# Converting eight instead of five float64 weight blocks during the attention

## The chip, the cores and the metric

The kernel runs on one core of a Trainium2 chip. The metric is the device time in microseconds (us) of one execution; the time of a kernel is the median of a few runs. Besides the times there is a profile of one execution: a page of views and a trace that can be queried. Engines are called as in the profile: PE is TensorE (PEld its weight loads), DVE is VectorE, ACT is ScalarE, POOL is GpSimd, and SP is SyncE, which issues most of the DMAs.

## The reference

Three stages follow one another: an attention with four sink keys and a window of 128 keys, a two-layer MLP with a PReLU, and a layer of eight experts with top-1 routing.

```
x = attention(q, k, v)              # 2 batches x 8 heads x 768 tokens x 64
x = x as (1536 tokens, 512)
h = x @ w_in                        # 512 -> 2048
g = max(h, 0) + alpha * min(h, 0)
x = g @ w_out                       # 2048 -> 512
e = argmax(x @ w_gate)              # one of 8 experts per token
out = gate * (max(x @ w1[e], 0) @ w2[e])
```

`w_in` and `w_out` come as float64; all the rest is float32.

## The kernel before

**Weights.** [...] Each of the two matrices is cut into eight blocks of 128x1024 values; the order of work is `wi0, wo0, wi1, wo1, ...`, sixteen blocks numbered 0 to 15. A block passes through three functions. `w_load` issues its DMA of 1 MB (1024 KB in the profile) on SP's queue into one of two raw buffers (two halves of `raw_all`). `w_convert` makes float32 of it: ACT takes an absolute value (L211 or L229), then DVE runs four instructions, a maximum (L216), a shift with a mask (L219), and two that merge bits of the high word (L224) and of the low word (L231). `w_convert_n(n)` converts block n and then issues the load of block n + 2, since the raw buffer is then free. `w_split` cuts the float32 block into a high and a low part, because every product is made of three float32r matmuls: ACT copies the high part (L259), and DVE or POOL subtracts (L262).

**Attention.** 48 units (2 batches x 4 pairs of heads x 6 query tiles of 128) go through a software pipeline written out by hand: pass n of a loop does the scores of unit n (L722, and all that belongs to it) together with the softmax of unit n - 1 (L737 on DVE, L741 on ACT), the transposes of unit n - 2 (L754), the product with the values of unit n - 6 (L832), the normalisation of two units that are 7 and 8 back (L843 to L850 on DVE), and two passes after that the transposes of the normalised tile (L797), which ACT and POOL (L811) then store as `x`. There are 59 passes; from pass 48 on no new unit enters, and the pipeline drains. In these last passes the first eight steps of the MLP are woven in (`next(mlp)`), four for each of its first two hidden tiles. Six units share one set of `ka` and `qa` tiles; SP loads the set of units 12 to 17 in pass 6, with two buffers for each.

**Early weights.** `early_weights` is a generator which converts blocks 0 to 4 during the attention, each in two halves, with seven stops per block. `EARLY = 32` lets it advance by one stop in each pass from n = 16 (48 - 32) on. The loads of blocks 0 and 1 are issued in passes 8 and 14. The first three blocks are also split there, the subtraction on POOL. SP's queue in the first passes further holds eight DMAs (`FILL_AT`) that write zeros to the table `xs` in device memory, 771 KB each.

**MLP.** Four blocks of tokens (512, 512, 256, 256), each with 16 hidden tiles f. Step f does 12 matmuls up (L350), 12 matmuls down for tile f - 2 (L381, in the first two blocks of tokens), and the activation: ACT L361 and L362, DVE L363, ACT L370, DVE L373. In the first block of tokens step f also converts weight block f + 3 (from f = 2 on) and splits weight block f + 2; later blocks of tokens only split. DVE works in the order of the program, in each such step: L216, L219, L363, L224, L231, L262, L373.

Of the kernel before, what the change touches and what calls it, by code (L numbers as in the profile page):

```python
# [35 lines left out]
def attention_mlp_moe_kernel(  # L36
# [19 lines left out]
    B, _, _, S = q.shape  # L56
    _, NG, _, GH, NQ, D1 = v.shape
# [130 lines left out]
    def w_load(n):  # L188

        if n >= len(worder):  # L190
            return
        nm, fg = worder[n]
        if nm == "wi":
            src = w_in_v[:, :, fg * FG * P * EW:(fg + 1) * FG * P * EW]
        else:
            src = w_out_v[:, fg * FG:(fg + 1) * FG, :]
        if wide_w:
            t = raw_all[:, n % 2 * 2 * SW:(n % 2 + 1) * 2 * SW]
        else:
            t = wres[nm, fg] = slot(f"{nm}{fg}", F32)  # L200
        nc.sync.dma_start(out=t.rearrange("p (a b) -> p a b", a=src.shape[1]), in_=src)
        wraw[nm, fg] = t

    def w_convert(nm, fg, parts=1):

        raw = wraw[nm, fg].rearrange("p (n t) -> p n t", t=2)
        lo, hi, hif = raw[:, :, 0], raw[:, :, 1], raw.bitcast(F32)[:, :, 1]
        w = wres[nm, fg] = slot(f"{nm}{fg}", F32)
        wb = w.bitcast(I32)
        cuts = [slice(o, o + SW // parts) for o in range(0, SW, SW // parts)]  # L210
        nc.scalar.activation(w[:, cuts[0]], hif[:, cuts[0]], AF.Abs)  # L211
        if parts > 1:
            yield
        for n, x in enumerate(cuts):

            nc.vector.tensor_scalar(  # L216
                out=w[:, x], in0=w[:, x], scalar1=TINY, scalar2=None, op0=ALU.max
            )
            nc.vector.tensor_scalar(  # L219
                out=wb[:, x], in0=wb[:, x], scalar1=3, scalar2=0x3FFFFFF8,  # L220
                op0=ALU.logical_shift_left, op1=ALU.bitwise_and,
            )
            yield
            nc.vector.scalar_tensor_tensor(  # L224
                out=wb[:, x], in0=hi[:, x], scalar=-0x40000000, in1=wb[:, x],
                op0=ALU.bitwise_and, op1=ALU.bitwise_or,
            )
            if n + 1 < parts:
                nc.scalar.activation(w[:, cuts[n + 1]], hif[:, cuts[n + 1]], AF.Abs)  # L229
            yield  # L230
            nc.vector.scalar_tensor_tensor(  # L231
                out=wb[:, x], in0=lo[:, x], scalar=29, in1=wb[:, x],
                op0=ALU.logical_shift_right, op1=ALU.bitwise_or,
            )
            if parts > 1:
                yield

    def w_convert_n(n, parts=1):

        if wide_w and n < len(worder):  # L240
            yield from w_convert(*worder[n], parts)
            w_load(n + 2)

    def w_split(n, parts=1):


        bl, m = divmod(n, len(worder))
        if bl >= NBLK:
            return
        nm, fg = worder[m]  # L250
        w = wres[nm, fg]
        r = 2 * (fg % 2) + (4 if nm == "wo" else 0)
        hi, lo = slot(f"r{r}"), slot(f"r{r + 1}")
        a = KD if nm == "wi" else FG
        wts[bl, nm, fg] = [t.rearrange("p (a b) -> p a b", a=a) for t in (hi, lo)]
        eng = nc.gpsimd if parts > 1 else nc.vector
        xs_ = [slice(o, o + SW // parts) for o in range(0, SW, SW // parts)]
        for x in xs_:
            nc.scalar.copy(hi[:, x], w[:, x])  # L259
            yield  # L260
        for x in xs_:
            eng.tensor_sub(lo[:, x], w[:, x], hi.bitcast(F32)[:, x])  # L262
            if parts > 1:
                yield
# [57 lines left out]
    ahead = wide_w and shared and NT // XB > 1 and PW <= 2 * P + 8  # L322
# [5 lines left out]
    def open_first():  # L328
        gp.append(mctx.enter_context(tc.tile_pool(name="gp", bufs=2, side="right")))
        slots_m = mctx.enter_context(tc.tile_pool(name="slots_m", bufs=1, side="right"))  # L330
        for n in (2, 3):
            slot_pool[f"r{n}"] = slots_m

    if ahead:
        open_first()
        for tag in ("wi2", "wo2"):
            slot_pool[tag] = slots_x

    nalpha = const.tile([P, KF], F32, name="nalpha")
# [45 lines left out]

    def convert_at(n):

        return iter(()) if ahead and n < 2 else w_convert_n(n + 3)

    def split_at(n):  # L390

        return iter(()) if ahead and n < 1 else w_split(n + 2)

    LAG = 2
    three = ((0, 0), (0, 1), (1, 0))


# [92 lines left out]
    def mlp_steps():  # L490
# [7 lines left out]
        def lower(part=None):  # L498
            pb, pf, pg = pending[0]
            ts = range(TBLK[pb][1] // P)  # L500
            if pf == 0:
                accs[pb] = [bank("t", f"acc{pb}_{t}", (P, DM)) for t in ts]
            mlp_down(pb, pf, wts[pb, "wo", pf // FG], pg, accs[pb], ts)
            pending.pop(0)
            if pf < KF - 1:
                return None
            routing = route(pb, ts, accs[pb], [])
            next(routing)
            return routing
# [4 lines left out]
        def down_to(t):  # L514

            for pb, pf, pg in pending:
                if pf not in first_down:
                    first_down.append(pf)
                    mlp_down(pb, pf, wts[pb, "wo", pf // FG], pg, accs[pb], [t])

        for bl in range(NBLK):
# [4 lines left out]
            for f in range(KF):  # L526
# [5 lines left out]
                if last and f == KF - 1:  # L532
                    down_to(0)
                elif len(pending) == LAG:
                    routing = lower() or routing
# [72 lines left out]
    with ExitStack() as actx:  # L608
# [264 lines left out]

        def early_weights():
            split = iter(())
            for n in range(5 if ahead else 0):
                for _ in w_convert_n(n, 2):
                    yield
                    next(split, None)
                for _ in split:  # L880
                    pass
                split = w_split(n, 2) if n < 3 else iter(())
            for _ in split:
                pass

        nu = len(units)
        assert NQ % 2 == 0 and NQ >= 6

        def at(xs, n):
            return xs[n] if 0 <= n < len(xs) else None  # L890
# [6 lines left out]
        for st in sts[1:QA]:  # L897
            load_qk(st)
        early = early_weights()
        nc.sync.dma_start(out=alpha_sb, in_=alpha)  # L900
        nc.sync.dma_start(out=wg_sb, in_=w_gate)
# [1 line left out]

        EARLY, MLP_AHEAD = 32, 8

        FILL_AT = (3, 5, 7, 10, 12, 15, 18, 20)

# [4 lines left out]
        for n in range(nu + 11):  # L914
            u = at(units, n)
            norm = iter(())
            if n % 2 == 0 and at(groups, (n - 8) // 2):
                norm = normalise(groups[(n - 8) // 2])
            if at(units, n - 1):
                softmax(units[n - 1], norm)  # L920
            for _ in norm:
                pass
            parts = {"T": p_transposes(units[n - 2]) if at(units, n - 2) else iter(())}
            parts["V"] = values(units[n - 6]) if at(units, n - 6) else iter(())
            for h in range(2):
                parts["QR"[h]] = scores(u, h) if u else iter(())
            for x in WEAVE:
                next(parts[x], None)
            for x in "TQRV":
                for _ in parts[x]:  # L930
                    pass
            if at(units, n - 2):
                p_evacuate(units[n - 2])
            if n % 2 == 0:
                late_transposes(at(groups, (n - 4) // 2), at(groups, (n - 10) // 2))
            elif at(groups, (n - 3) // 2):
                sink_gather(groups[(n - 3) // 2])
            if u:
                st = u.t.st
                sn = st.b * (H // 2) + st.hp  # L940
                s2 = at(sts, sn + 2)
                if u.i == 0 and sn > 0 and at(sts, sn + QA - 1):
                    load_qk(sts[sn + QA - 1])
                if u.i == 1 and st.hp % 2 == 0 and s2:
                    load_v(s2.b, s2.hp // 2)
            if n in FILL_AT:
                next(table, None)
            if ahead and n in (nu - EARLY - 8, nu - EARLY - 2):
                w_load(int(n > nu - EARLY - 8))
            if n == nu - EARLY:  # L950
                nc.vector.tensor_scalar(
                    out=nalpha, in0=alpha_sb, scalar1=-1.0, scalar2=None, op0=ALU.mult
                )
            if n >= nu - EARLY:
                next(early, None)
            if n >= nu and ahead and n_ahead < MLP_AHEAD:
                next(mlp)
                n_ahead += 1
# [433 lines left out]
```

## Time and profile before

| what | before |
|---|---|
| median of 3 runs | 612.49 us (611.35 to 613.03) |
| profiled execution | 612.21 us, its span 610.4 us |
| PE busy | 587.4 us (96%) |
| DVE busy | 396.6 us (65%) |
| ACT busy | 346.6 us (57%) |
| mean granted clock of PE | 0.997 |
| DMA | 81.76 MB, 134 GB/s on average |

The span reaches from the first to the last instruction of the profiled execution; its own time has 1.8 us more around it. PE is nearly always busy, but its matmuls are pipelined and a matmul that waits inside the pipeline also counts as busy, so idle time of PE and the distance between the starts of its matmuls are read together. The attention fills the first 122 us or so, the first block of tokens of the MLP the stretch to about 204 us.

### The profile page before, as it was taken

Reading aid. Unit: us, or ns where it says so; the run is one execution under the profiler, and the core shown is the slowest. Engines: PE = TensorE matmul, PEld = TensorE weight load, DVE = VectorE, ACT = ScalarE, POOL = GpSimd, SP = SyncE. Lnnn points to the kernel's source line nnn. Section 1 sums busy time; section 2 is a strip of 40 time slices with the busy share of each in tenths; the row PEclk is TensorE's granted clock in tenths of the full one; section 3 lists DMA queues with packets and bytes.
Section 4 is the critical chain, followed back from the end, with each engine's and each line's share of the span. In section 5 each row is a group of like instructions: output and inputs, shape, how many; then the busy total and the mean of one; then the engine's idle time right before and its main releaser. Section 6 shows DMA issues by size and latency. Waiting matters only on the chain. (4 is left out here: it accounts for less than half of the span.)

```text
span 610.4 us, 9113 instructions
## 1 busy us (share of the span) xinstructions
PE 587.4 (96%) x3230; PEld 491.7 (81%) x3230; DVE 396.6 (65%) x788; ACT 346.6 (57%) x642; POOL 100.0 (16%) x134
## 2 busy tenths in 40 slices
PE   7999999999989999999999999999999999999994
PEld 5999998888767888888899898877777777778783
DVE  5678788589999454454565786976326583985250
ACT  4677776476565354434564676854327574675330
POOL 5011423210000000003000020112220431332031
PEclk9999999999999999999999999999999999999998
DMA  7969741225559000001000011334928593993000
GB/s 220 327 206 300 226 126 70 70 69 169 176 159 389 4 0 1 2 0 53 17 1 2 18 67 35 127 99 128 335 69 307 200 356 126 310 381 141 17 21 34
DMA packets 32404, 81.76 MB, mean 134 GB/s; under 512 B 3574, under 2 KB 4134, under 8 KB 32352
## 3 DMA queue, kind: packets, MB, share of 16 engines
q1 hardware_dynamic: 28208, 69.54, 34.6%
q0 software_dynamic: 4144, 11.53, 5.2%
q8 instruction: 31, 0.51, 0.3%
q14 instruction: 21, 0.17, 0.1%
HBM read 66.65 MB, written 16.29 MB: 136 GB/s over the span
## 5 line engine op out<-in xcount | busy, mean ns | idle before, releaser
L350 PE MATMUL h<-x,r 128*128 128x512 f32 (+1 forms) x768 | 149.2, 341 | 3.2 <-DVE r L262 3.1
L350 PEld LDWEIGHTS h<-x,r 128*128 128x128 f32 x768 | 120.1, 189 | 22.3 <-DVE r L262 5.2
L381 PE MATMUL acc<-r,gh 128*128 128x512 f32 x384 | 120.5, 395 | 0.0
L381 PEld LDWEIGHTS acc<-r,gh 128*128 128x128 f32 x384 | 69.9, 188 | 14.3
L381 PE MATMUL acc<-r,gl 128*128 128x512 f32 x192 | 75.9, 395 | 0.0
L363 DVE SCALAR_TENSOR_TENSOR g<-gn,nalpha,g 128x512 f32<-128x512 f32 (+1 forms) x64 | 39.3, 615 | 47.6 <-ACT g L362 47.6
L722 PE MATMUL s<-ka,qa 128*128 128x260 f32 x192 | 60.3, 401 | 4.5 <-DMA qa<-in_q_dram 4.2
L361 ACT ACTIVATE gn<-h 128x512 f32<-128x512 f32 (+1 forms) x64 | 31.4, 490 | 53.6 <-PE h L350 53.4
L832 PEld LDWEIGHTS o<-vr,pT 128*128 128x128 f32 x352 | 55.6, 192 | 4.8
L1104 POOL DMA_INDIRECT xs<-x,slot_i x12 | 14.0, 1166 | 272.1 <-DVE run L1120 151.2
L262 DVE TENSOR_TENSOR r<-wo,r 128x1024 fp32r<-128x1024 f32 x31 | 37.9, 1224 | 27.6 <-ACT r L259 27.4
L832 PE MATMUL o<-vr,pT 128*128 128x65 f32 x352 | 53.6, 251 | 0.0
L1219 ACT ACTIVATE hh<-et 128x512 f32<-128x512 f32 x26 | 15.6, 599 | 65.3 <-PE et L1214 58.8
L741 ACT ACTIVATE p<-sx,mn 128x260 f32<-128x260 f32 (+1 forms) x96 | 42.9, 487 | 10.1 <-DVE mn L737 9.6
L259 ACT CAST r<-wo 128x1024 fp32r<-128x1024 f32 (+1 forms) x33 | 33.8, 1023 | 22.6 <-PE acc L381 21.7
L754 PE MATMUL pt<-ident,p 128*128 128x128 f32 x176 | 46.5, 279 | 0.0
L737 DVE CUSTOM_DVE_ANT_0 sx<-s,mask 128x260 f32<-128x260 f32 (+1 forms) x96 | 36.8, 399 | 14.4 <-PE s L722 8.7
L370 ACT CAST gh<-g 128x512 fp32r<-128x512 f32 (+1 forms) x64 | 33.0, 516 | 20.9 <-DVE g L363 20.7
L381 PEld LDWEIGHTS acc<-r,gl 128*128 128x128 f32 x192 | 36.1, 188 | 8.6
L262 DVE TENSOR_TENSOR r<-wi,r 128x1024 fp32r<-128x1024 f32 x30 | 36.6, 1222 | 3.6 <-ACT r L259 3.4
L373 DVE TENSOR_TENSOR gl<-g,gh 128x512 fp32r<-128x512 f32 (+1 forms) x64 | 35.3, 551 | 1.6 <-ACT gh L370 1.6
L722 PEld LDWEIGHTS s<-ka,qa 128*128 128x128 f32 x192 | 31.2, 201 | 5.6 <-issue 4.2
(200 smaller groups left out, 1104.0 us busy)
## 6 DMA issues: line engine op xcount, KB each, us to landing
raw_all<-in_w_dram SPq DMA_DIRECT2D x36, 512.0 KB, 5.9
more_raw<-in_w_dram SPq DMA_DIRECT2D x28, 512.0 KB, 6.5
raw_all<-in_w_in_dram SPq DMA_DIRECT2D x8, 1024.0 KB, 5.4
raw_all<-in_w_out_dram SPq DMA_DIRECT2D x8, 1024.0 KB, 5.7
xs<-r SPq DMA_DIRECT2D x8, 771.0 KB, 10.6
rows<-xs POOLq DMA_DIRECT2D x20, 256.0 KB, 5.7
vr<-in_v_dram SPq DMA_DIRECT2D x4, 780.0 KB, 5.5
out_dram<-fill SPq DMA_DIRECT2D x2, 1536.0 KB, 11.4
```

The source lines that it names most:

```text
L259: nc.scalar.copy(hi[:, x], w[:, x])
L262: eng.tensor_sub(lo[:, x], w[:, x], hi.bitcast(F32)[:, x])
L350: nc.tensor.matmul(ph[:, :TB], wi[wl][:, kk, f0:f0 + P], xT_at(kk, tok, TB, xl), start=(n == 0), stop=(n == 3 * KD - 1),)
L363: nc.vector.scalar_tensor_tensor(out=g, in0=gn, scalar=nalpha[:, f:f + 1], in1=g, op0=ALU.mult, op1=ALU.add)
L370: nc.scalar.copy(gh, g)
L373: nc.vector.tensor_sub(gl, g, gh.bitcast(F32))
L381: nc.tensor.matmul(acc[t], g[a][:, t * P:(t + 1) * P], wo[w][:, f % FG, :], start=(f == 0 and x == 0), stop=(f == KF - 1 and x == 2),)
L722: nc.tensor.matmul(s[:, o:o + w], st.qa[:, h, toks], st.ka[:, c:c + w], start=True, stop=True, skip_group_check=True,)
L737: nc.vector.tensor_tensor_reduce(out=x[:, :w], in0=u.s[h][:, :w], in1=m[:, :w], scale=-scale, scalar=BIG, op0=ALU.add, op1=ALU.min, accum_ ...
L741: nc.scalar.activation(t.p[:, u.ii, h, :w], x[:, :w], AF.Exp, bias=t.mn[:, c:c + 1], scale=-1.0)
L754: nc.tensor.transpose(pt[:, c * P:(c + 1) * P], t.p[:, u.ii, h, u.offs[n]:u.offs[n] + P], ident,)
L832: nc.tensor.matmul(t.o[:, 2 * u.ii + h, :], u.pT[:, w], vr[:, hv * NQ + j, :], start=(not sg and n == 0), stop=(n == len(js) - 1), skip_gr ...
```

## The change

Eight blocks instead of five are converted in the attention: `LEAD = 6` replaces the 3 in `convert_at`, and `early_weights` runs over `LEAD + 2` blocks. It starts at pass 10 instead of 16 (`EARLY = 38`) and advances by two stops in each pass from n = 48 on. The loads of blocks 0 and 1 hang on the same constant and so are issued in passes 2 and 8. Blocks 8 to 15 are left to the MLP, in its steps f = 2 to 9. Two more slots (`wi3`, `wo3`) are taken from the pool that exists during the attention.

```
-        for tag in ("wi2", "wo2"):
+        for tag in ("wi2", "wo2", "wi3", "wo3"):
             slot_pool[tag] = slots_x
...
-        return iter(()) if ahead and n < 2 else w_convert_n(n + 3)
+        return iter(()) if ahead and n < 2 else w_convert_n(n + (LEAD if ahead else 3))
...
     LAG = 2
+
+    LEAD = 6
...
-            for n in range(5 if ahead else 0):
+            for n in range(LEAD + 2 if ahead else 0):
                 for _ in w_convert_n(n, 2):
...
-        EARLY, MLP_AHEAD = 32, 8
+        EARLY, MLP_AHEAD = 38, 8
...
-            if n >= nu - EARLY:
+            for _ in range((n >= nu - EARLY) + (n >= nu)):
                 next(early, None)
```

The two loads outside the generator stand in the same loop and are not edited: `if ahead and n in (nu - EARLY - 8, nu - EARLY - 2): w_load(...)`.

## Rows read from the trace of the kernel before

**Rows 1.** The page: its head, and the rate of the DMAs in 40 slices.
```profile
span 610.4 us, 9113 instructions
...
GB/s 220 327 206 300 226 126 70 70 69 169 176 159 389 4 0 1 2 0 53 17 1 2 18 67 35 127 99 128 335 69 307 200 356 126 310 381 141 17 21 34
```
**Rows 2.** Waits of PE, whole span: us in total, times, longest us.
```profile
PE h L350 <- DVE r L262: 3.1, 4, 0.9
...
PE pk_x L797 <- DVE xn L850: 0.9, 1, 0.9
```
**Rows 3.** Timeline of PE, late steps of the first MLP block: start us, us.
```profile
179.95 0.62 PE L350 MATMUL h<-x,r 128*128 128x512 f32 x2
181.31 2.56 PE L350 MATMUL h<-x,r 128*128 128x512 f32 x10 [0.74 <-DVE r L262]
...
192.02 0.63 PE L350 MATMUL h<-x,r 128*128 128x512 f32 x2
193.56 2.60 PE L350 MATMUL h<-x,r 128*128 128x512 f32 x10 [0.91 <-DVE r L262]
...
204.43 2.91 PE L350 MATMUL h<-x,r 128*128 128x512 f32 x12
```
**Rows 4.** Timeline of DVE, the same instruction in two steps running.
```profile
158.61 0.75 DVE L363 SCALAR_TENSOR_TENSOR g<-gn,nalpha,g 128x512 f32<-128x512 f32 x1
...
164.74 0.74 DVE L363 SCALAR_TENSOR_TENSOR g<-gn,nalpha,g 128x512 f32<-128x512 f32 x1
```
**Rows 5.** Busy us in one stretch: PE, PEld, DVE, ACT, POOL, then clock, DMA.
```profile
155.00:196.00 41.00, 37.88 (x161) 29.50 (x159) 40.59 (x48) 24.79 (x34) 0.00 (x0) 1.00 0.67 233
```
**Rows 6.** Waits of DVE: two of 109.9 to 126.7 us, then one of 40 to 123.
```profile
DVE g L363 <- ACT g L362: 5.3, 2, 3.0
DVE den L843 <- PE o L832: 1.5, 1, 1.5
...
DVE wi L216 <- ACT wi L211: 2.4, 2, 1.3
```
**Rows 7.** Timeline of DVE, second half of weight block 4.
```profile
109.89 0.41 DVE L216 TENSOR_SCALAR wi<-wi 128x512 f32<-128x512 f32 x1
110.33 0.83 DVE L219 TENSOR_SCALAR wi<-wi 128x512 int32<-128x512 int32 x1
111.20 0.69 DVE L224 SCALAR_TENSOR_TENSOR wi<-raw_all,wi 128x512 int32<-128x512 int32 x1
...
112.63 0.68 DVE L231 SCALAR_TENSOR_TENSOR wi<-raw_all,wi 128x512 int32<-128x512 int32 x1
```
**Rows 8.** Timeline of POOL at the same place.
```profile
110.14 0.74 POOL L811 TENSOR_TENSOR x<-xn,x 128x256 fp32r<-128x256 f32 x1 [2.70 <-ACT xn L810]
```
**Rows 9.** Timeline of PE: first scores of units 12, 18 and 24.
```profile
27.09 0.60 PE L722 MATMUL s<-ka,qa 128*128 128x260 f32 x2
...
40.48 0.60 PE L722 MATMUL s<-ka,qa 128*128 128x260 f32 x2
...
53.89 0.60 PE L722 MATMUL s<-ka,qa 128*128 128x260 f32 x2
```
**Rows 10.** Timeline of SP, issues of DMAs in passes 6 to 8.
```profile
14.14 2.53 SPq L695 DMA_DIRECT2D qa<-in_q_dram  x2
16.72 0.61 SPq L155 DMA_DIRECT2D xs<-r  x1
17.37 0.60 SPq L201 DMA_DIRECT2D raw_all<-in_w_in_dram  x1
```
**Rows 11.** DMA issues at 14.1, 15.4, 16.8, 17.4 us: KB, us to landing.
```profile
qa<-in_q_dram SPq DMA_DIRECT2D x1, 192.0 KB, 10.4
...
qa<-in_q_dram SPq DMA_DIRECT2D x1, 192.0 KB, 9.8
...
xs<-r SPq DMA_DIRECT2D x1, 771.0 KB, 10.6
...
raw_all<-in_w_in_dram SPq DMA_DIRECT2D x1, 1024.0 KB, 12.8
```

## The prediction, made before the changed kernel ran

> **What bounds the kernel now.** I read the page first, then PE's list of waits, then the first block of the MLP and the attention one engine at a time, and last the DMA issues. The reader is to see that PE sets the end nearly everywhere, and that the conversions matter at one place. PE's list of waits has one entry that a conversion causes: four waits of the up matmuls for the low part of a split `wi` block (L262), 3.1 us in all [rows 2]. They lie in the first block of tokens, at f = 8, 10, 12 and 14. There DVE has more work per step than PE. DVE's period is 164.74 - 158.61 = 6.13 us [rows 4], and it is busy for 40.59 of 41 us [rows 5]; PE needs, without a wait, (204.43 - 193.56 + 0.48) / 2 = 5.7 us for a step [rows 3], where 0.48 us stands for the two matmuls that run ahead of the wait (12 in 2.91 us, 0.24 each). So DVE falls behind by 0.45 us a step from f = 2 on, first eats its lead, and from f = 8 on PE pays at every second step, when a new `wi` block is due. The two later payments are 181.31 - 179.95 - 0.48 = 0.88 us and 193.56 - 192.02 - 0.48 = 1.06 us [rows 3], 1.9 us together.
>
> In the attention PE is the bound and the conversions cost nothing: six units take 40.48 - 27.09 = 13.39 us almost without conversions and 53.89 - 40.48 = 13.41 us with them [rows 9]. That holds as long as DVE's instructions fit beside the softmax, as they do at one stop per pass.
>
> **The change, part by part.**
>
> *Steps f = 10 to 12 lose their conversion.* Steps f = 2 to 9 still convert, eight instead of eleven, so DVE falls behind in the same way up to f = 9. The low part that is due at f = 10 is made in step 8, behind seven conversions, before as after. What goes are the waits at f = 12 and 14: a gain of 1.9 us. The waits at f = 8 and 10 stay. More than the 3.1 us of all four waits [rows 2] is not to be had here, and whatever makes DVE arrive later at f = 2 is passed on in full to the up matmuls at f = 10, since DVE has no idle time in between.
>
> *The last passes of the attention get DVE work.* With one stop per pass from n = 10, blocks 0 to 4 end in pass 44 and three stops of block 5 in pass 47. At two per pass, the rest of block 5 falls into passes 48 and 49, block 6 into 50 to 53 and block 7 into 53 to 56. For DVE that is five half blocks and one L231. A half block costs 0.41 + 0.43 + 0.69 + 0.68 = 2.2 us by durations [rows 7], with L219 undisturbed as below, 2.1 us as the starts overlap a little; so 5 x 2.1 + 0.65 = 11.1 us come. What leaves these passes is the second half of block 4, 0.41 + 0.83 + 0.69 + 0.68 = 2.6 us [rows 7], now done six passes earlier. Net 8.5 us. DVE's room there is its waits, 5.3 + 1.5 = 6.8 us [rows 6]. Not all of it can be used: in pass 50 the two calls issue ACT's absolute value of block 6 and DVE's maximum that reads it, one behind the other, and DVE stands in line until ACT is through the copies of that pass. The longest such wait in the trace is 1.3 us [rows 6]; I take 1.0. So 8.5 - 5.8 = 2.7 us do not fit, and with half a collision with POOL more (below), DVE reaches f = 2 about 2.9 us late. Bounds: 1.2 us (halves at 2.0 us, all 6.8 us used) and 4.4 us (halves at 2.2 us, the 1.3 us wait, two more collisions of 0.4 us). Queued behind these DVE instructions are the last normalisation, for which PE already waits 0.9 us [rows 2] and will wait about 1 us longer, and the activations of tiles 0 and 1. PE's own loss there is not added: it lies inside the 2.9 us, which come due at f = 6 to 10 anyway.
>
> Both parts together: 2.9 - 1.9 = +1.0 us (-0.7 to +2.5).
>
> *The start at pass 10 instead of 16.* The pattern of early stops against the six units of a set is the same, shifted by exactly one set, so I take blocks 0 to 4, their splits and their collisions at no cost; the cover is PE's 13.4 us per set [rows 9]. Had DVE no room there, each block would cost up to its 4.2 us.
>
> *The loads of blocks 0 and 1 in passes 2 and 8.* They pass other DMAs on SP's queue. The load of pass 2 is now issued ahead of two zero fills and ahead of `ka` and `qa` of units 12 to 17. The DMAs of this queue land in the order of issue: the fill issued at 16.72 lands at 27.3, the load issued at 17.37 at 30.2 [rows 10, 11]. Thus the megabyte itself takes 2.9 us, and `qa`, landed now at 14.14 + 10.4 = 24.5 us and, its second half issued 1.2 us later, at 15.3 + 9.8 = 25.1 us, would land at 27.4 and 28.0. The scores need the first half at 27.09 [rows 9] and the second 0.66 us later. So PE loses 0.3 to 0.4 us, and nothing behind gives it back, since PE is the bound there. The other end: at the mean rate of the first slice, 220 GB/s [rows 1], the megabyte takes 4.8 us and PE loses 2.1 us. If the fills give way, nothing. I take 0.5 us, near the row of the load itself. The load of pass 8 stands where that of block 0 stood, and the later ones come between loads with more slack; nothing for these.
>
> Sum: +1.0 + 0.5 = +1.5 us. The profiled execution took 612.21 us (span 610.4 [rows 1], 1.8 around it), so 613.7; the median of the runs lies 0.28 us above that execution, so 614.0 us against the median.
>
> **A rule weighed.** L219 takes 0.83 us beside the POOL instruction of 110.14 us and 0.43 alone [rows 7, 8]: a collision costs 0.4 us of the 0.74 that POOL works. The Trainium skill, SBUF — State Buffer, section "SBUF: two separate sides", says more: the port pair of VectorE and GpSimd is an exclusive lock held for a whole instruction, and the loser blocks entirely. By the row one more collision is 0.4 us; by the rule it can be the full 0.74, which in this trace no L219 of 110 us shows, because POOL had started 0.2 us before it.
>
> **The rivals.**
>
> *Faster: DVE's gaps swallow the tail.* If DVE comes to f = 2 on time, because its waits of the last passes [rows 6] are room in full and ACT hands over without delay, and if the early load hides, the waits at f = 12 and 14 go for nothing in return: -1.9 us, 610.6; if 1.0 us is left over, 611.6. For it: 6.8 us of room stand against 8.5 us of work. Against it: the room has to lie where the work is. It decides for "faster" only when less than about 0.1 us is left over, which is why most of this case is "same". Chance 0.22 (0.14 faster, 0.08 same).
>
> *Slower by far: POOL blocks DVE in the tail.* Passes 50 to 56 hold four POOL instructions of 0.74 us like the one of [rows 8], now each beside a conversion. If each stops DVE for its whole length, the tail grows by 4 x 0.74 = 3.0 us instead of my 0.2: +4.3 us, 616.8. Against it: most conversions in the attention meet POOL without PE losing anything. Chance 0.10, slower. This is the case of the rule above.
>
> *The early load is hidden.* If the megabyte of pass 2 overlaps with the fills or a set of `qa` is not late, only +1.0 us is left: 613.5. Chance 0.15 (0.14 same).
>
> **Chances and range.** My forecast has 0.53. A measurement of this kernel can tell about 0.3%, 1.84 us, from no change: 610.65 to 614.33. The forecast lies inside, near the upper edge, with its own range 612.6 to 615.8; I put 0.31 of it on "same" and 0.22 on "slower". Together: faster 0.14, same 0.31 + 0.08 + 0.14 = 0.53, slower 0.22 + 0.10 + 0.01 = 0.33. The range 611.0 to 616.4 leaves out the better half of the first rival and most of the second, about 0.2.
>
> **What would show it right or wrong.** In the profile after: a wait of PE's scores for `qa` near 27 us of some tenths; the sets of six units after it again at 13.4 us; no DVE wait of a microsecond between 113 and 127 us except one for ACT's L211; the last L797 about 1 us later; a first PE wait for L262 already at f = 6, further ones at f = 8 and 10 of about 1 us, and none after; the up matmuls of the second token block at about 206 us instead of 204.43. I am wrong if DVE still shows free microseconds in the last passes (then faster), if the scores of unit 12 wait for 1 to 2 us or DVE instructions there stretch beside POOL (then slower).

## The result and the profile after

The changed kernel took 615.17 us (median of 8 runs, 613.97 to 617.16) against 612.13 us for the kernel before (8 runs, 611.06 to 613.03). The ratio is 1.0059, with a 95% interval of 1.0046 to 1.0071: 3.6 us slower by the ratio (the two medians alone differ by 3.0). The span of the profiled execution is 613.9 us instead of 610.4. Lines of the attention and behind it stand two further down than before (L722 is L724, L797 is L799, L811 is L813, L850 is L852).

PE's list of waits after, over the whole span (us in total, times, longest):

```profile
PE pk_x L799 <- DVE xn L852: 2.5, 1, 2.5
...
PE h L350 <- DVE r L262: 2.0, 3, 0.9
PE s L724 <- DVE xn L852: 1.0, 1, 1.0
```

Beside [rows 2], three things are to be seen. The waits for a low part fell from four to three, and from 3.1 to 2.0 us. The wait of the last transpose grew from 0.9 to 2.5 us. And a new wait stands ahead of scores. The timeline of PE shows that it is the first scores of unit 12; those of units 18 and 24 follow below it, and the last scores of unit 11 stand above:

```profile
26.52 0.60 PE L724 MATMUL s<-ka,qa 128*128 128x260 f32 x2
...
28.67 0.68 PE L724 MATMUL s<-ka,qa 128*128 128x260 f32 x2 [0.97 <-DVE xn L852]
...
42.14 0.60 PE L724 MATMUL s<-ka,qa 128*128 128x260 f32 x2
...
55.54 0.60 PE L724 MATMUL s<-ka,qa 128*128 128x260 f32 x2
```

Against [rows 9] unit 12 is 1.58 us late and unit 24 is 1.65 us late; the two sets between take 13.47 and 13.40 us, so the loss is carried through the attention as it is. Not all of it is a wait. In the trace of before, the last scores of unit 11 started here:

```profile
26.07 0.60 PE L722 MATMUL s<-ka,qa 128*128 128x260 f32 x2
```

PE was thus 0.45 us late already ahead of unit 12. It was as late at 10.19 us (9.74 before), when the early load had not been issued yet, so this part is a difference between two executions and not of the change: in the thirteen profiles of this case these scores start anywhere from 24.86 to 26.52 us. From there to unit 12 it is 28.67 - 26.52 = 2.15 us instead of 27.09 - 26.07 = 1.02, and 1.13 us is the wait.

What ended the wait is `qa`. The profile puts it down to DVE's `xn`, which ended at 28.65 us, but `xn` is a result of the attention that the scores do not read. In the profile of a later run with the same order of DMAs (spare matmuls for PE, below) the same wait carries the name of `qa`:

```profile
28.16 0.68 PE L724 MATMUL s<-ka,qa 128*128 128x260 f32 x2 [1.44 <-DMA qa<-in_q_dram]
```

These are SP's issues of DMAs after (start, time to issue), and then the KB and the time to landing of the load, of the second fill, of `ka` and of the first `qa`:

```profile
11.27 0.42 SPq L201 DMA_DIRECT2D raw_all<-in_w_in_dram  x1
11.88 1.78 SPq L155 DMA_DIRECT2D xs<-r  x2
14.19 0.93 SPq L692 DMA_DIRECT2D ka<-in_k_dram  x1
15.16 1.29 SPq L697 DMA_DIRECT2D qa<-in_q_dram  x2
```
```profile
raw_all<-in_w_in_dram SPq DMA_DIRECT2D x1, 1024.0 KB, 9.3
...
xs<-r SPq DMA_DIRECT2D x1, 771.0 KB, 13.0
...
ka<-in_k_dram SPq DMA_DIRECT2D x1, 396.0 KB, 14.0
qa<-in_q_dram SPq DMA_DIRECT2D x1, 192.0 KB, 13.4
```

The first `qa` lands at 15.16 + 13.4 = 28.56 us, just ahead of the scores, instead of 14.14 + 10.4 = 24.54 [rows 10, 11]: 4.0 us later, not 2.9.

The end of the attention and the first steps of the MLP, on PE's timeline:

```profile
125.08 0.41 PE L799 MATMUL pk_x<-ident,xn 128*128 128x128 f32 x2 [2.48 <-DVE xn L852]
125.25 4.59 PE L350 MATMUL h<-x,r 128*128 128x512 f32 x12
...
132.49 2.97 PE L350 MATMUL h<-x,r 128*128 128x512 f32 x12
...
150.17 2.60 PE L350 MATMUL h<-x,r 128*128 128x512 f32 x10 [0.38 <-DVE r L262]
...
162.43 2.58 PE L350 MATMUL h<-x,r 128*128 128x512 f32 x10 [0.76 <-DVE r L262]
...
174.68 2.62 PE L350 MATMUL h<-x,r 128*128 128x512 f32 x10 [0.90 <-DVE r L262]
...
179.94 2.97 PE L350 MATMUL h<-x,r 128*128 128x512 f32 x12
...
207.87 2.88 PE L350 MATMUL h<-x,r 128*128 128x512 f32 x12
```

The lines are the start of f = 2 behind the last transpose, f = 3, the waits at f = 6, 8 and 10, step f = 11, and the second token block. The waits stand at f = 6, 8 and 10 and nowhere after. The second token block (the last line) begins at 207.87 us instead of 204.43 [rows 3], 3.44 us late, and that distance stays to the end of the span (3.5 us). In the trace of before, the up matmuls of f = 2 and of f = 11 are these:

```profile
122.03 3.05 PE L350 MATMUL h<-x,r 128*128 128x512 f32 x12
...
174.32 2.97 PE L350 MATMUL h<-x,r 128*128 128x512 f32 x12
```

One thing was not foreseen: the twelve up matmuls of f = 2 took 4.59 us instead of 3.05. The windows of after give the reason (us of the stretch, busy us and instructions of PE, PEld, DVE, ACT, POOL, then the granted clock, and the DMAs' share and GB/s):

```profile
120.00:123.00 3.00, 2.60 (x14) 1.80 (x12) 2.28 (x4) 1.21 (x3) 0.47 (x1) 1.00 0.01 3
123.00:124.00 1.00, 0.00 (x0) 0.00 (x0) 1.00 (x2) 1.00 (x4) 0.04 (x1) 1.00 0.00 0
124.00:125.00 1.00, 0.00 (x0) 0.00 (x0) 0.86 (x5) 0.46 (x1) 0.71 (x1) 1.00 0.00 0
125.00:126.00 1.00, 0.92 (x5) 0.85 (x6) 0.93 (x3) 0.47 (x2) 0.00 (x0) 0.98 0.65 96
126.00:129.00 3.00, 3.00 (x8) 2.30 (x7) 2.90 (x5) 2.09 (x4) 1.40 (x3) 0.50 0.87 312
129.00:130.00 1.00, 1.00 (x5) 0.80 (x4) 0.97 (x3) 0.00 (x0) 0.00 (x0) 0.81 0.04 16
```

PE stood still for 2.5 us ahead of the last transpose, and then ran at 1.2 instead of 2.4 GHz from 126 to 129 us.

The same stretch on DVE's timeline, the instructions that count:

```profile
112.59 0.85 DVE L219 TENSOR_SCALAR wo<-wo 128x512 int32<-128x512 int32 x1
...
116.34 0.48 DVE L216 TENSOR_SCALAR wi<-wi 128x512 f32<-128x512 f32 x1 [0.64 <-ACT wi L211]
...
119.92 0.84 DVE L219 TENSOR_SCALAR wi<-wi 128x512 int32<-128x512 int32 x1
...
122.83 0.69 DVE L373 TENSOR_TENSOR gl<-g,gh 128x512 fp32r<-128x512 f32 x1 [0.69 <-ACT gh L370]
...
126.49 1.11 DVE L231 SCALAR_TENSOR_TENSOR wo<-raw_all,wo 128x512 int32<-128x512 int32 x1
...
132.26 0.69 DVE L216 TENSOR_SCALAR wi<-wi 128x1024 f32<-128x1024 f32 x1
```

The last line is the first conversion of step f = 2. In the trace of before that is this line:

```profile
126.66 0.69 DVE L216 TENSOR_SCALAR wo<-wo 128x1024 f32<-128x1024 f32 x1
```

So DVE is 5.6 us late, 3.95 beyond the attention's 1.65. The two waits shown, 0.64 and 0.69 us, are all that is left of DVE's idle time in the tail. Two L219 and one L231 take 0.41 to 0.42 us more than their own time (0.43 and 0.69 us); beside each of them POOL runs L813, as in [rows 7, 8].

PE's starts say the same: at f = 11, behind the three waits, it is 179.94 - 174.32 = 5.62 us late, the attention's 1.65 and DVE's 3.95. Behind that, the two waits that are gone give 2.2 us back.

So the account of the profiled execution is 0.45 (an earlier difference between the two executions) + 1.2 (late `qa`) + 3.95 (DVE late at f = 2) - 2.2 (the two waits that are gone) = 3.4 us.

### The profile page after: what moved, and what is told of

Its sections match the earlier page's. It is cut to its first block, busy times and chain, and to the rows that moved or that the text cites. A ratio compares the mean times of both kernels' runs of the same rounds, so it can differ in the third digit from the quotient of the medians.

```text
span 613.9 us, 9120 instructions
## 1 busy us (share of the span) xinstructions
PE 589.5 (96%) x3230; PEld 493.1 (80%) x3230; DVE 399.0 (65%) x800; ACT 346.3 (56%) x645; POOL 100.5 (16%) x134
## 5 line engine op out<-in xcount | busy, mean ns | idle before, releaser
L724 PE MATMUL s<-ka,qa 128*128 128x260 f32 x192 | 60.7, 404 | 5.6 <-DMA qa<-in_q_dram 4.2
L724 PEld LDWEIGHTS s<-ka,qa 128*128 128x128 f32 x192 | 31.3, 202 | 6.8 <-issue 4.2
```

Source lines behind the costliest of these rows:

```text
L724: nc.tensor.matmul(s[:, o:o + w], st.qa[:, h, toks], st.ka[:, c:c + w], start=True, stop=True, skip_group_check=True,)
```

## The experiments

A short name for a measure that is used below: the *MLP stretch* runs from the start of the up matmuls of f = 2 to those of the second token block. It is 204.43 - 122.03 = 82.40 us before and 207.87 - 125.25 = 82.62 after. The run with the fewest of these waits has 78.80.

**The fills behind `qa`.** The changed kernel with the zero fills in later passes.

```
-        FILL_AT = (3, 5, 7, 10, 12, 15, 18, 20)
+        FILL_AT = (7, 8, 9, 10, 12, 15, 18, 20)
```

> The changed kernel, with its first three zero fills issued in passes 7, 8 and 9 instead of 3, 5 and 7, so that the early weight load and the keys and queries of unit 12 have the DMA queue to themselves. Theory A (the megabyte of pass 2 pushes back the queries of unit 12, and nothing gives this back): the scores of unit 12 start near 27.1 us instead of 28.67, the attention ends 1.6 us earlier, and the ratio to the kernel before falls from 1.0059 to about 1.003. Rival (the DVE work from pass 10 on is what slows the attention): unit 12 and the time stay as in the changed kernel, 1.006.

Measured: 613.66 us, ratio 1.0033 (1.0022 to 1.0043). Unit 12 starts at 26.73 us without a wait, 1.01 us behind the last scores of unit 11. So 0.0026 of the ratio, 1.6 us, was the early load, and the rest, 2 us, is the *tail*, the last passes of the attention with the work that they hand on to the MLP.

**The loads alone.** The kernel before, with only its two loads moved to passes 2 and 8.

```
-            if ahead and n in (nu - EARLY - 8, nu - EARLY - 2):
-                w_load(int(n > nu - EARLY - 8))
+            if ahead and n in (2, 8):
+                w_load(int(n > 2))
```

> The kernel before, with nothing but the loads of weight blocks 0 and 1 moved from passes 8 and 14 to passes 2 and 8. Theory A: the scores of unit 12 wait for the queries until about 28.6 us, and the time rises by 1.5 us, ratio 1.0025. Rival (the loads are hidden, the early conversions cost): no change, 1.000, unit 12 at 27.1 us.

Measured: 613.01 us, ratio 1.0025 (1.0014 to 1.0035), 1.5 us. In its profile the first half of unit 12 starts at 27.22 and the second waits for `qa` until 28.20, 0.98 instead of 0.66 us behind it. Unit 13 is 0.53 us later than in the trace of before, and 0.14 of that stood already at unit 11, so the wait cost this execution only 0.4 us. Its first `qa` landed at 14.27 + 12.7 = 26.97 us, against 28.56 in the changed kernel: the moment of landing differs from execution to execution. Both runs together put the early load at 1.5 to 1.6 us by the medians, and undoing it and doing it alone agree.

**PE fed across its wait.** Ten spare matmuls into a free bank, ahead of the transposes in the pass that PE waits in; they compute nothing that is used.

```
+        def warm_up(k):
...
+            if n == nu + 8:
+                warm_up(10)
```

> The changed kernel with ten more up matmuls into an unused PSUM bank (0.23 us each, nobody reads their result) right ahead of the last transposes, so that PE has work in the 2.5 us in which it waits for DVE there. Theory B (DVE sets the time of this stretch until f = 10, so PE's half clock at 126 to 129 us is paid out of time that PE would have waited anyway): the granted clock stays at its upper level there, PE waits instead at f = 4 and 6, and the time stays at 1.006 within 0.001. Rival (the 1.5 us lost at half clock are a loss of their own): the ratio falls by 0.0025 to about 1.0035.

PE's timeline of this kernel:

```profile
121.95 2.45 PE L891 MATMUL warm_up<-x,r 128*128 128x512 f32 x10
124.60 0.41 PE L799 MATMUL pk_x<-ident,xn 128*128 128x128 f32 x2 [0.20 <-DVE xn L852]
124.77 3.04 PE L350 MATMUL h<-x,r 128*128 128x512 f32 x12
```

The clock stays at 1.00 and the twelve up matmuls take 3.04 us again. But the MLP stretch is 207.35 - 124.77 = 82.58 us, against 82.62 with the half clock: the 1.5 us come back as more waits for low parts (four, 3.3 us, instead of three, 2.0). While DVE is the one that is late, a slower PE only waits less. Of the first experiment the same can be said: there the clock did not fall after the same wait of 2.48 us, and its stretch is 205.83 - 123.23 = 82.60. As a whole the run took 617.62 us (ratio 1.0096, 1.0081 to 1.0112), 2.3 us more than the changed kernel, which neither theory had. Its profile shows 1.3 us of it in one wait of the expert stage near 494 us (2.08 instead of 0.77 us). The other kernel with these matmuls (below) has the same long wait, 2.27 us near 490 us, and the same kernel without them has 0.77, so it goes with the spare matmuls; why they should lengthen it is open.

**Six blocks.** One block more than before instead of three, one stop per pass throughout, the fills behind `qa` (`FILL_AT` as in the first experiment).

```
-    LEAD = 6
+    LEAD = 4
...
-            for _ in range((n >= nu - EARLY) + (n >= nu)):
+            for _ in range(n >= nu - EARLY):
```

> The changed kernel with six blocks ahead (LEAD = 4), one stop per pass throughout, and the zero fills moved as in the first run. The last passes then hold four stops as before the change. Theory C (what costs is the work put into the last passes, not conversions ahead as such): DVE reaches f = 2 as early as before, steps f = 2 to 11 convert, the wait at f = 14 goes and the other three stay: 1.0 us faster than before, ratio 0.998. Rival (any further block ahead delays the attention): 1.000 or above.

Measured: 610.54 us, ratio 0.9980 (0.9970 to 0.9989). The last transpose waits 0.9 us as before, DVE's waits in the tail are still there (5.3 us for L362), three waits for low parts remain (2.2 us), and the stretch is 203.57 - 122.34 = 81.23 us. One conversion less costs nothing here and gains a wait.

**The same six blocks with the fills where they were.**

```
-        FILL_AT = (7, 8, 9, 10, 12, 15, 18, 20)
+        FILL_AT = (3, 5, 7, 10, 12, 15, 18, 20)
```

> Six blocks ahead with the zero fills where they were, in passes 3, 5 and 7. Theory A: the early load pushes back the queries of unit 12 again, unit 12 starts at about 28.5 us, and 1.0 to 1.5 us of the gain of six blocks are given back, ratio 1.000 to 1.0005. Rival (moving the fills did something else): 0.998.

Measured: 611.95 us, ratio 1.0003 (0.9992 to 1.0014): 1.4 us more than with later fills. The early load alone eats what a block gains.

**Seven blocks at one stop per pass.** The six blocks with fills behind `qa`, and one more.

```
-    LEAD = 4
+    LEAD = 5
```

> Seven blocks ahead (LEAD = 5), one stop per pass from pass 10 to 58, zero fills moved as before. The last passes hold eleven stops instead of the three of the kernel before and the eighteen of the changed one. Theory C (the tail has about 6.8 us of DVE room, and each half block there costs 2.3 us): eight stops more are 5 us of work, so DVE reaches f = 2 between 0 and 1.5 us late, the wait at f = 14 goes: between 1.0 faster and 0.5 us slower than before, ratio 0.9985 to 1.001, worse than with six blocks. Rival (the two stops per pass, not the amount, made DVE late): as with six blocks or better, 0.998 or below.

Measured: 614.59 us, ratio 1.0042 (1.0029 to 1.0056), outside what I had expected. DVE's timeline of this kernel:

```profile
118.10 0.75 DVE L363 SCALAR_TENSOR_TENSOR g<-gn,nalpha,g 128x512 f32<-128x512 f32 x1 [3.57 <-ACT g L362]
...
120.60 0.83 DVE L219 TENSOR_SCALAR wi<-wi 128x512 int32<-128x512 int32 x1
...
123.94 1.30 DVE L219 TENSOR_SCALAR wi<-wi 128x512 int32<-128x512 int32 x1
...
129.10 0.69 DVE L216 TENSOR_SCALAR wo<-wo 128x1024 f32<-128x1024 f32 x1
```

DVE idles for 3.57 us and is late all the same. Its first conversion of step f = 2 (the last line) comes 2.44 us later than in the trace of before, although unit 12 started 1.22 us earlier (25.87): 3.7 us late. In front of the long wait no stop is ready. The one stop of that pass is ACT's absolute value for block 6, which stands behind copies that wait for PE and starts at 116.41 us; DVE's first instruction of that block is the next stop (120.15 us) and queues behind the activation. That stop then comes ahead of the last normalisation, for which the last transpose waits 2.64 us, and the rest of the block behind it, ahead of f = 2. Two more L219 meet POOL (0.83 and 1.30 us). So the rate of two stops is not what made the tail late, as one of the theories had it: idle time in the tail can't be summed up and filled, it has to lie where a stop is ready.

**The tail alone.** The kernel before, its start and its loads kept, with eight blocks and three stops per pass in the drain.

```
-            for n in range(5 if ahead else 0):
+            for n in range(8 if ahead else 0):
...
-            if n >= nu - EARLY:
+            for _ in range((n >= nu - EARLY) + 2 * (n >= nu)):
```

> The kernel before with eight blocks ahead, started in pass 16 with the loads in passes 8 and 14 as before, and three stops per pass from pass 48 on: all of the additional work lies in the last passes, 24 stops instead of the changed kernel's 18. Theory C: nothing is lost up to pass 48 (unit 12 at 27.1 us), DVE reaches f = 2 about 8 us late, two waits of 1.9 us go: 5 to 7 us slower than before, ratio 1.008 to 1.012. Rival (the tail is room enough, and the loads alone cost): 0.997.

Measured: 618.12 us, ratio 1.0101 (1.0085 to 1.0116). Unit 12 starts at 26.62 us without a wait, and the last transpose now waits 4.91 us. More of the same work in the tail makes more of the same loss, without any early load.

**Three steps free.** The changed kernel, its eight late conversions in steps f = 5 to 12.

```
-        return iter(()) if ahead and n < 2 else w_convert_n(n + (LEAD if ahead else 3))
+        return iter(()) if ahead and n < 5 else w_convert_n(n + 3)
```

> The changed kernel, with its eight MLP conversions in the steps f = 5 to 12 instead of f = 2 to 9, so that DVE has three steps with no conversion behind the tail. Theory A (what the tail costs comes due through DVE, and only as long as DVE is the bound): DVE catches up its 4 us in f = 2 to 4, the waits of the up matmuls at f = 6, 8 and 10 go, and at most one or two come back at f = 12 and 14, 0.3 to 1.3 us; what stays is the late `qa` (+1.65), the later last transpose (+1.6) and, if PE's clock falls again, about 1.5 us that now nothing absorbs, less the 3.1 us of waits of the kernel before: +1.9 to +2.9 us with the half clock, +0.4 to +1.4 without, so a ratio of 1.003 to 1.005, or 1.0005 to 1.0025. Theory B (PE itself loses the 4 us in the tail, by the transpose and the half clock, and DVE's lateness is only a sign of it): the waits at f = 6 to 10 stay in part, ratio 1.005 or above.

**The same, with PE fed across its wait** (the ten matmuls of above).

> As the run before it, with ten spare matmuls ahead of the last transposes, so that PE doesn't stand still there. In the changed kernel these matmuls gained nothing in this stretch, because PE paid for the half clock out of time that it would have waited for DVE. Theory A: here DVE no longer sets the time, so if the clock fell in the run before, this run is 1.5 us shorter from the third hidden tile on (0.9975 of it). Theory B (half a clock for some microseconds costs nothing in either kernel): the two have the same time from there on, within 0.3 us. If the clock does not fall in the run before, both theories give the same, and the run tells only whether the spare matmuls themselves cost anything, above all near 494 us, where they went with a stray wait of PE before.

Measured: 612.81 us, ratio 1.0006 (0.9994 to 1.0018), and 614.15 us, ratio 1.0044 (1.0023 to 1.0065). PE's timeline of the first, and then of the second:

```profile
123.94 4.49 PE L350 MATMUL h<-x,r 128*128 128x512 f32 x12
131.17 2.98 PE L350 MATMUL h<-x,r 128*128 128x512 f32 x12
...
186.83 2.92 PE L350 MATMUL h<-x,r 128*128 128x512 f32 x12
...
194.82 2.61 PE L350 MATMUL h<-x,r 128*128 128x512 f32 x10 [1.83 <-DVE r L262]
```
```profile
123.81 3.05 PE L350 MATMUL h<-x,r 128*128 128x512 f32 x12
129.51 2.97 PE L350 MATMUL h<-x,r 128*128 128x512 f32 x12
...
185.18 2.92 PE L350 MATMUL h<-x,r 128*128 128x512 f32 x12
...
191.99 2.60 PE L350 MATMUL h<-x,r 128*128 128x512 f32 x10 [0.65 <-DVE r L262]
```

The lines are f = 2, 3, 13 and 14. With three steps to catch up in, DVE's lateness vanishes: no wait is left at f = 6 to 12. Now the half clock is PE's own loss. From f = 2 to f = 3 the first kernel takes 7.23 us and the second 5.70, and at f = 13 the 1.5 us are still there. So in these two profiles whether the slow clock costs anything depends on who is late: nothing in the changed kernel, 1.5 us here. The times do not confirm it: the fed kernel was to be 1.5 us shorter, and its median is 1.3 us longer. Its runs spread from 611.68 to 619.36 us, and the profiled one was the fastest; the wait near 490 us takes 1.5 us of that back even there, the rest is open. The wait at f = 14 is 1.2 us longer in the first kernel, as the load of that block took 7.7 us to land instead of 5.5 and ACT's L211, for which DVE waits, stood until then; why the load took longer is open.

**Three steps free and the fills behind `qa`** (both edits of above, without the spare matmuls).

> The first of these runs with the zero fills behind `qa` (passes 7, 8, 9, 10, 12, 15, 18, 20). Theory A: the attention's 1.65 us go too, down to about 0.3, so 1.0 to 1.4 us less than the first run: a ratio of about 0.9985 to 1.001. Rival: the later fills collide with loads that this order of conversions needs early, and the gain is under 0.5 us.

Measured: 611.62 us, ratio 0.9988 (0.9975 to 1.0000), 1.1 us below the run with the fills early. Unit 12 starts at 27.06 us.

**One step free.** The six blocks with fills behind `qa`, and no conversion in step f = 6; blocks 10 to 15 follow one step later each.

```
-        return iter(()) if ahead and n < 2 else w_convert_n(n + (LEAD if ahead else 3))
+        return iter(()) if ahead and (n < 2 or n == 6) else w_convert_n(n + (LEAD - (n > 6) if ahead else 3))
```

> Six blocks ahead as above, and step f = 6 of the first MLP block converts nothing; steps 2 to 5 convert blocks 6 to 9 and steps 7 to 12 blocks 10 to 15. Theory D (PE waits because DVE falls behind by 0.45 us a step, so one step without the 3.7 us of a conversion, put ahead of the first wait, clears all of them): no PE wait for L262 is left, 2.7 us less than with six blocks alone, ratio about 0.9935. Rival (DVE's period is not what sets these waits, but when each block arrives): the waits stay, 0.998.

Measured: 607.76 us, ratio 0.9936 (0.9922 to 0.9949), 3.9 us faster than the kernel before and the best of all. PE's waits of this kernel, and the two ends of its MLP stretch:

```profile
PE pk_x L799 <- DVE xn L852: 0.9, 1, 0.9
...
PE h L350 <- DVE r L262: 0.4, 1, 0.4
```
```profile
121.57 3.05 PE L350 MATMUL h<-x,r 128*128 128x512 f32 x12
...
200.37 2.91 PE L350 MATMUL h<-x,r 128*128 128x512 f32 x12
```

The stretch is 200.37 - 121.57 = 78.80 us, 3.6 less than before. Against the run with six blocks above, the same conversions are made early and only the free step lies elsewhere (f = 6, not f = 12). One block moved into the attention without disturbing the tail is enough, if the step that it frees lies ahead of the first wait: DVE gets a whole block's time back there, where the lateness that all later waits are made of is built up.

## Why the prediction came out as it did

The mechanism was right, and the time lay in the range, but two terms of the sum were too small, so that the likeliest case, no measurable change, gave way to slower. The prediction had named two signs of that: scores of unit 12 that wait for 1 to 2 us, and DVE instructions that stretch beside POOL. Both came.

*Steps f = 10 to 12 lose their conversion: right.* The waits are at f = 6, 8 and 10, none at f = 12 and 14; gain 2.2 us where I had 1.9. The list of waits holds only PE's idle time, and a step with a wait loses more than that: step f = 12 took 186.49 - 179.95 = 6.54 us before and takes 5.54 now, 1.00 us for a wait of 0.74; f = 14 took 6.79 and takes 5.62. For the same reason PE's step without a wait is 5.6 us, not 5.7 (f = 2 to 8 before, (155.64 - 122.03) / 6), and DVE falls behind by 0.53 us a step, not 0.45. So it was wrong too that more than the 3.1 us of the list is not to be had: the MLP stretch with one step free is 3.6 us shorter.

*The start at pass 10: right.* Sets of 13.47 and 13.40 us with the early stops.

*The early load, "I take 0.5 us": the step that failed most for its size.* It costs 1.6 us when undone and 1.5 us when done alone. The order of landing was right; the price of the megabyte was too low on the whole. I took 2.9 us from the distance of two landings late in this queue. In the early stretch, where all of the queue's transfers are still in flight, `qa` was 4.0 us later in the changed kernel and 2.4 with the loads alone. At the mean rate of the changed kernel's stretch from 8 to 18 us, 291 GB/s, the megabyte would take 3.6 us, an estimate between my two rows of 2.9 and 4.8. As 2.5 us are slack ahead of PE, a little more delay makes a multiple of the loss: 0.5 us forecast, 1.1 in the one profile, 1.5 to 1.6 by the medians. The Trainium skill, DMA: Bandwidth & Descriptors, section "Queues, rings and completion order", says that each DMA engine takes descriptors in the order of the ring; the trace agrees, as everything issued behind the load landed later, `ka` after 14.0 and `qa` after 13.4 us.

*DVE "about 2.9 us late": 3.95, inside the bounds 1.2 to 4.4.* Three terms were off. A half block takes 2.25 us, not 2.1 (124.85 to 127.52 us less 0.42, and 127.52 to 129.76), since an instruction that reads the one before it starts 0.73 us after it, not 0.60 (L224 to L231, 117.32 to 118.05): 5 x 0.15 = 0.75 us. "Half a collision with POOL" were three of 0.41 to 0.42 us (L219 at 112.59 and 119.92, L231 at 126.49), 1.25 instead of 0.2 us. The other way, DVE's idle time shrank by 6.4 us where I had 5.8 (7.7 us with the small waits that [rows 6] leave out, to 1.3; ACT's L211 took 0.64, not 1.0). By that 2.9 + 0.75 + 1.05 - 0.6 = 4.1, against 3.95 measured; that it lay inside the bounds owes something to the third term, which ran against the other two. What the collisions cost is read from durations; no run takes POOL's work out of the tail. The collisions are the rival of POOL in small: it did come, but not at its price of 3.0 us. The rule weighed there, that of the exclusive lock (the Trainium skill, SBUF — State Buffer, section "SBUF: two separate sides"), is neither shown nor refuted by it: the L219 of 112.59 began 0.23 us after a POOL instruction of 0.79 us, and lost 0.42 where the rule would have let it stand for the remaining 0.56, and the two others lost as much of 0.54 and 0.56; but the profile's spans on POOL are rough.

*"PE's own loss there is not added": right, and for more than I had thought of.* The last transpose came 1.6 us later instead of 1, and the clock's fall added 1.5 us on PE, yet both lie inside DVE's 3.95 us. The fed run shows that for the clock. For the forecast this was luck: it had no fall of the clock in it, and 1.5 us on PE stayed free of charge only because DVE was late by more.

*The rival "faster"* had half of its reason met: DVE's waits were in fact filled, down to 1.3 us. Its condition, DVE on time at f = 2, was not: the work was more than the room, and the collisions, the longer halves and the load came on top.

*Not in the sum at all:* 0.45 us of the profiled difference, by which PE was late before the change could act. It belongs to the comparison of two single profiles; whether the medians hold any of it is not shown.

## What to carry to other kernels

A big load that is moved ahead in a full queue delays every small one behind it. Price it with the rate of that place (here 291 GB/s, 3.6 us for the megabyte, against 2.4 to 4.0 seen), not with a distance of landings read elsewhere, and take off only the slack that is left; or move something that nobody waits for behind the small ones in exchange. Idle time of an engine in a pipeline's drain is room only where its next instruction is ready, and the work put there can land beside another engine that slows it, as here beside POOL. Before two profiles are compared at one place, see whether they were level ahead of it. Where one engine falls behind by a little in every step, a step freed ahead of the first wait gains more (0.9936) than one freed at the end (0.9980).

## What the runs showed of the hardware

- PE stood still for 2.48 us before the last transpose in the changed kernel and in the run with later fills. In the one the granted clock then was 0.50 from 126 to 129 us (1.2 GHz), in the other it stayed at 1.00. So the length of the wait alone does not settle it. It also fell to 0.50 behind the waits of 2.47 and 2.48 us in the two kernels with three steps free and no spare matmuls, of 2.64 us with seven blocks and of 4.91 us with the tail alone, and behind none of the five waits of 0.9 us. With ten matmuls of 2.45 us in all in that gap it stayed at 1.00 (2.4 GHz) both times that they were tried.
- The twelve up matmuls of f = 2 take 3.04 to 3.05 us at 2.4 GHz and 4.49 to 4.77 us in the five profiles in which the clock fell.
- With the same order of DMAs ahead of it, `qa` held up the first half of unit 12 by 1.13, 1.60 and 0.17 us in three profiles (the changed kernel, the fed one, three steps free), counted from the last scores of unit 11 less the 1.01 to 1.02 us without a wait. One profile of such a wait is not its price; pairs of medians gave 1.1 to 1.6 us.
